# Attention and two FFN layers on one core: float64 words to float32 in two VectorE operations, with a leaky relu for the rescaling

## The chip, the cores and the metric

The kernel runs on one core of a Trainium2 chip. The metric is the device time of one execution in microseconds (us), as the median of several runs. The engines are named as in the profile: PE is TensorE's matmul and PEld its weight load, DVE is VectorE, ACT is ScalarE, POOL is GpSimd, SP is SyncE, which here only issues transfers.

## The reference, cut to what matters

Three layers follow each other. The attention pools keys and values over eight positions, and its result, 4608 tokens of 512 features, goes through two feed-forward layers:

```python
x = attention(q, pooled(k), pooled(v))        # 4608 x 512
h = np.maximum(x @ w_in, 0.0)                 # 512 x 2048
x = (s * (h * h) + b) @ w_out                 # 2048 x 512
gate = 1.0 / (1.0 + np.exp(-(x @ w_gate)))    # 512 x 1536
out = (gate * (x @ w_val) @ w_out2).astype(np.float32)
```

The five weight matrices arrive as float64, the rest as float32.

## The kernel before, in words

The tokens are nine blocks of 512. For the first layer, five blocks (0, 1, 2, 4, 6) go through `emit_h` and `emit_x`, one group of 128 hidden columns at a time (16 groups a block, so 80 steps), and the other four go in pairs through `first_half`, `second_half` and `emit_o`, where seven half-sized products take the place of eight; all of the second layer goes that way too. Each matmul is made of three: the operands are split by `split` (L55, L56) into a rounded high part, which ACT writes, and a remainder, which DVE (for activations) or POOL (for weights) subtracts.

No operation of the kernel works on float64. A weight arrives as 64-bit words in a `raw` tile (128 x 512 of them, 512 KB, loaded by SP at L73), and `convert` makes float32 of it. It sees the tile as two strided views, `low` and `high`, of 32-bit words. ACT reads `high` as a float32 and multiplies it by 2^-112 into `w` (L86), which sets the exponent to the float32 bias and leaves room for a shift. DVE shifts `low` right by 29 in place (L87), then shifts `w` left by 3 and joins the three bits of `low` (L88), which pushes out the sign, and at last takes the sign bit of `high` and joins it (L89). The converted weight then goes to `split`.

There are 68 conversions. Of these, 32 are the 16 groups of `w_in` and of `w_out`, which `split_wi` and `split_wo` convert during block 0, when each step of PE needs a new group of both; the other 36 are weights of the second layer, converted ahead of use by `prep_gate`, `prep_val` and `prep_out`: 12 of them between other work of the first layer's later blocks, 24 in the first layer's paired blocks.

The order of instructions on an engine: the opening (attention of the first two units and the first conversions) stands in the order of the code. From there a planner at build time orders the engines by its own estimates of cost, and from step 16 on PE, and to the end of the steps SP, keep the order of the code, while DVE, ACT and POOL stay with the planner. `raw` has three buffers, so a load waits until a conversion three earlier is done with its tile.

Of the kernel before, what the change touches and what calls it, by code (L numbers as in the profile page):

```python
# [8 lines left out]
F32 = mybir.dt.float32  # L9
F32R = mybir.dt.float32r  # L10
I32 = mybir.dt.int32
ACTF = mybir.ActivationFunctionType
ALU = mybir.AluOpType
# [6 lines left out]
def pooled_attention_two_ffn(ctx, tc, q, k, v, v_left, w_in, w_out, s_in, b_in, w_gate, w_val, w_out2, out):  # L20
# [8 lines left out]
    nc = tc.nc  # L29
# [49 lines left out]
    def convert(raw, w):  # L79

        words = raw.rearrange("p (f two) -> p f two", two=2)
        low, high = words[:, :, 0], words[:, :, 1]
        nc.scalar.activation(out=w.bitcast(F32), in_=high.bitcast(F32), func=ACTF.Copy, scale=2.0**-112)  # L86
        nc.vector.tensor_scalar(out=low, in0=low, scalar1=29, scalar2=None, op0=ALU.logical_shift_right)  # L87
        nc.vector.scalar_tensor_tensor(out=w, in0=w, scalar=3, in1=low, op0=ALU.logical_shift_left, op1=ALU.bitwise_or)  # L88
        nc.vector.scalar_tensor_tensor(out=w, in0=high, scalar=-(2**31), in1=w, op0=ALU.bitwise_and, op1=ALU.bitwise_or)  # L89
        return w.bitcast(F32)  # L90

    def block_of(t):
# [42 lines left out]
    def split_wi(i):  # L135
        if i >= M1:
            return
        w = convert(wi_raw.pop(i), cv_tile())
        t = wi_tile(i)
        split(t[:, 0], t[:, 1], w, nc.gpsimd)  # L140
        later.append((w1d[i], t))
        later.append((w6d[i // 2][:, 0:512] if i % 2 else w6d[i // 2][:, 512:1024], w))
# [12 lines left out]
    def split_wo(m):  # L155
        if m < M1:
            t = wo_p.tile([128, 2, DM], F32R, name=f"wo{m}")
            split(t[:, 0], t[:, 1], convert(wo_raw.pop(m), cv_tile()), nc.gpsimd)
            wo[m] = t
# [11 lines left out]
    def prep_gate(m):  # L171
        prep["gt"] = convert(prep["g"], cv_tile())
# [750 lines left out]
```

## Time and profile before

| | us |
|---|---|
| median of 3 runs | 1774.92 |
| lowest and highest run | 1774.47 and 1777.0 |
| the profiled execution | 1777.24 |
| its span, first to last instruction | 1775.4 |
| PE busy | 1718.1 |
| PEld busy | 1435.0 |
| DVE busy | 996.1 |
| ACT busy | 873.2 |
| POOL busy | 702.8 |

The span is what the trace shows, and 1.84 us lie around it. Busy times of different engines overlap. The mean granted clock of PE over the span is 0.988 of full speed.

### The profile page before, as it was taken

How to read it: one execution, taken by the hardware profiler on the slowest of the kernel's cores; microseconds unless marked ns; L12 is line 12 of the kernel's file. 1: busy time of each engine (PE TensorE's matmuls, PEld its weight loads, DVE VectorE, ACT ScalarE, POOL GpSimd, SP SyncE). 2: the span in 40 equal slices, each digit the busy share in tenths (PEclk: the TensorE clock that was granted, in tenths of full speed). 3: DMA queues.
4: the chain of work that ended last, by engine and by line, in shares of the span. 5: the costliest groups of instructions: out<-in, count | busy, mean ns of one | idle time of the engine just before them, and what ended most of it. 6: DMA issues, size and time to landing. Idle time of an engine off the chain costs nothing.

```text
span 1775.4 us, 22857 instructions
## 1 busy us (share of the span) xinstructions
PE 1718.1 (97%) x8184; PEld 1435.0 (81%) x8184; DVE 996.1 (56%) x1621; ACT 873.2 (49%) x1628; POOL 702.8 (40%) x788
## 2 busy tenths in 40 slices
PE   5889999999999999999999999999999999999998
PEld 4777888788888878877888888888888888888898
DVE  7997555646642597469554454554455444545354
ACT  3666565556555666436653443344434343444244
POOL 4764335455310266336431434133413431443264
PEclk7999999999999999999999999999999999999999
DMA  6876558887444567687475334633463347233753
GB/s 240 298 239 217 180 209 314 276 289 247 175 160 129 197 247 257 228 288 248 173 242 170 117 127 158 222 119 123 152 235 119 110 148 251 102 118 138 250 183 122
DMA packets 98433, 347.01 MB, mean 195 GB/s; under 512 B 11408, under 2 KB 16528, under 8 KB 98320
## 3 DMA queue, kind: packets, MB, share of 16 engines
q1 hardware_dynamic: 90512, 319.33, 52.4%
q0 software_dynamic: 7808, 26.22, 4.2%
q8 instruction: 65, 1.06, 0.2%
q14 instruction: 48, 0.39, 0.1%
HBM read 278.40 MB, written 67.11 MB: 195 GB/s over the span
## 4 chain that ended last, share of the span: by engine, by line
PE 53%; DMA 4%; DVE 2%; issue 2%; POOL 2%; ACT 0%; DVEq 0%; POOLq 0%; SPq 0%; ACTq 0%
PE acc L819 20%; PE pc L723 6%; PE pc L724 6%; PE pc L725 6%; PE pb L725 5%; PE pb L724 5%; PE pb L723 5%; DMA wo<-wo2d 1%; DMA raw<-in 1%; POOL w L56 1%; DMA cv<-x1d 1%; POOL raw L180 1%; DVE raw L87 0%; DMA wo2d<-raw 0%; DVE cv L88 0%
## 5 line engine op out<-in xcount | busy, mean ns | idle before, releaser
L56 POOL TENSOR_TENSOR w<-w 128x256 fp32r<-128x256 f32 (+1 forms) x380 | 369.7, 1006 | 607.6 <-ACT w L55 579.3
L729 DVE TENSOR_TENSOR wk<-pc,wk 128x512 f32<-128x512 f32 (+1 forms) x304 | 196.2, 645 | 319.5 <-PE pc L725 318.9
L723 PE MATMUL pc<-xo,w 128*128 128x512 f32 (+1 forms) x608 | 228.4, 376 | 9.1 <-DVE wk L729 8.9
L724 PE MATMUL pc<-xo,w 128*128 128x512 f32 (+1 forms) x608 | 227.0, 373 | 0.0
L725 PE MATMUL pc<-xo,w 128*128 128x512 f32 (+1 forms) x608 | 226.9, 373 | 0.0
L55 ACT ACTIVATE w<-w 128x256 fp32r<-128x256 f32 (+1 forms) x380 | 157.5, 490 | 100.0 <-DMA w<-w7d 90.9
L56 DVE TENSOR_TENSOR gl<-g,gh 128x512 fp32r<-128x512 f32 (+1 forms) x172 | 133.1, 774 | 96.6 <-ACT gh L55 91.0
L723 PE MATMUL pb<-xo,w 128*128 128x512 f32 (+1 forms) x456 | 169.9, 373 | 1.4 <-ACT g L752 1.1
L725 PE MATMUL pb<-xo,w 128*128 128x512 f32 (+1 forms) x456 | 170.0, 373 | 1.1 <-POOL w L56 1.1
L724 PE MATMUL pb<-xo,w 128*128 128x512 f32 (+1 forms) x456 | 169.8, 372 | 0.0
L55 ACT ACTIVATE gh<-g 128x512 fp32r<-128x512 f32 (+1 forms) x172 | 105.7, 615 | 124.4 <-DVE g L744 122.0
L819 PE MATMUL acc<-wo,s 128*128 128x512 f32 x648 | 150.7, 390 | 0.9 <-DMA wo<-wo2d 0.6
L819 PEld LDWEIGHTS acc<-wo,s 128*128 128x128 f32 x648 | 121.3, 188 | 27.7 <-DMA wo<-wo2d 2.5
L723 PEld LDWEIGHTS pc<-xo,w 128*128 128x128 f32 x608 | 114.9, 189 | 33.4 <-DVE wk L729 13.6
L223 PE MATMUL hps<-xl,wi 128*128 128x512 f32 (+1 forms) x328 | 132.8, 405 | 3.1 <-ACT wi L55 2.5
L819 PE MATMUL acc<-wo,gh 128*128 128x512 f32 x432 | 133.1, 389 | 0.0
L725 PEld LDWEIGHTS pc<-xo,w 128*128 128x128 f32 x608 | 114.9, 189 | 20.3
L724 PEld LDWEIGHTS pc<-xo,w 128*128 128x128 f32 x608 | 115.0, 189 | 19.6
L251 PE MATMUL acc<-gl,wo 128*128 128x512 f32 x320 | 128.4, 401 | 2.4 <-DVE gl L56 2.4
L225 PE MATMUL hps<-xh,wi 128*128 128x512 f32 (+1 forms) x328 | 129.3, 394 | 0.0
L224 PE MATMUL hps<-xh,wi 128*128 128x512 f32 (+1 forms) x328 | 128.8, 393 | 0.0
L253 PE MATMUL acc<-gh,wo 128*128 128x512 f32 x320 | 125.3, 392 | 0.0
(126 smaller groups left out, 3415.4 us busy)
## 6 DMA issues: line engine op xcount, KB each, us to landing
wo<-wo2d SPq DMA_DIRECT2D x108, 512.0 KB, 4.0
w<-w7d SPq DMA_DIRECT2D x60, 896.0 KB, 4.4
raw<-in SPq DMA_DIRECT2D x68, 512.0 KB, 4.8
wi<-w1d SPq DMA_DIRECT2D x64, 512.0 KB, 4.0
wo<-wo1d SPq DMA_DIRECT2D x64, 512.0 KB, 4.6
w<-w6d SPq DMA_DIRECT2D x16, 896.0 KB, 5.9
kv<-in SPq DMA_DIRECT2D x24, 512.0 KB, 6.3
kv<-in SPq DMA_DIRECT2D x16, 576.0 KB, 6.0
```

The source lines that it names most:

```text
L55: nc.scalar.activation(out=hi, in_=src, func=ACTF.Copy)
L56: eng.tensor_tensor(out=lo, in0=src, in1=hi.bitcast(F32), op=ALU.subtract)
L223: nc.tensor.matmul(out=ps[:, f], lhsT=hi[:, kk], rhs=c[:, kk, f], start=kk == 0, stop=False)
L224: nc.tensor.matmul(out=ps[:, f], lhsT=hi[:, kk], rhs=a[:, kk, f], start=False, stop=False)
L225: nc.tensor.matmul(out=ps[:, f], lhsT=lo[:, kk], rhs=a[:, kk, f], start=False, stop=kk == KD - 1)
L251: nc.tensor.matmul(out=acc[j][d], lhsT=hi[:, f], rhs=gl, start=m == 0, stop=False)
L253: nc.tensor.matmul(out=acc[j][d], lhsT=lo[:, f], rhs=gh, start=False, stop=m == M1 - 1)
L723: nc.tensor.matmul(out=ps, lhsT=w[:, 0, x, kk], rhs=r[:, 1, kk, :n], start=first and kk == 0, stop=False, skip_group_check=True)
L724: nc.tensor.matmul(out=ps, lhsT=w[:, 0, x, kk], rhs=r[:, 0, kk, :n], start=False, stop=False, skip_group_check=True)
L725: nc.tensor.matmul(out=ps, lhsT=w[:, 1, x, kk], rhs=r[:, 0, kk, :n], start=False, stop=kk == 1, skip_group_check=True)
L729: nc.vector.tensor_tensor(out=o, in0=ps, in1=b_, op=ALU.add)
L819: nc.tensor.matmul(out=a, lhsT=l, rhs=r, start=m == 0 and first == 0, stop=m == M - 1 and first == 2)
```

## The change

In `convert` the rescaling on ACT becomes a leaky relu with slope 2^32 for negative inputs: a negative word comes out 2^32 times larger than a positive one of the same size, which sets one more bit of its exponent. The shift left by 3 moves that bit into the sign's place. So the DVE operation that fetched the sign from `high` (L89) falls away. Nothing else is edited; `high` is read by ACT alone now.

```diff
         words = raw.rearrange("p (f two) -> p f two", two=2)
         low, high = words[:, :, 0], words[:, :, 1]
-        nc.scalar.activation(out=w.bitcast(F32), in_=high.bitcast(F32), func=ACTF.Copy, scale=2.0**-112)
+        nc.scalar.activation(out=w.bitcast(F32), in_=high.bitcast(F32), func=ACTF.Prelu, scale=2.0**-112, alpha=2.0**32)
         nc.vector.tensor_scalar(out=low, in0=low, scalar1=29, scalar2=None, op0=ALU.logical_shift_right)
         nc.vector.scalar_tensor_tensor(out=w, in0=w, scalar=3, in1=low, op0=ALU.logical_shift_left, op1=ALU.bitwise_or)
-        nc.vector.scalar_tensor_tensor(out=w, in0=high, scalar=-(2**31), in1=w, op0=ALU.bitwise_and, op1=ALU.bitwise_or)
         return w.bitcast(F32)
```

## Rows read from the trace of the kernel before

**Rows 1.** Page, part 1: busy time, share of the span, instructions.

```profile
PE 1718.1 (97%) x8184; PEld 1435.0 (81%) x8184; DVE 996.1 (56%) x1621; ACT 873.2 (49%) x1628; POOL 702.8 (40%) x788
```

**Rows 2.** Windows: stretch, its length, busy time by engine, granted clock, transfers.

```profile
50.00:96.00 46.00, 36.40 (x191) 29.18 (x192) 44.53 (x60) 28.57 (x53) 36.98 (x30) 0.97 0.88 311
96.00:150.00 54.00, 50.21 (x229) 41.19 (x228) 50.25 (x76) 38.20 (x68) 29.14 (x26) 0.90 0.71 237
150.00:600.00 450.00, 444.70 (x2309) 375.95 (x2308) 238.29 (x446) 263.29 (x467) 160.96 (x200) 1.00 0.63 214
600.00:850.00 250.00, 239.84 (x1038) 194.62 (x1037) 177.92 (x242) 145.86 (x255) 135.09 (x145) 0.99 0.73 252
850.00:1776.00 926.00, 918.65 (x4281) 768.77 (x4279) 450.83 (x724) 381.46 (x756) 320.87 (x355) 1.00 0.47 160
```

**Rows 3.** Timeline of TensorE, 74 to 135 us: start, duration, idle before, releaser.

```profile
74.06 0.50 PE L251 MATMUL acc<-gl,wo 128*128 128x512 f32 x1 [2.41 <-DVE gl L56]
...
95.02 0.66 PE L445 MATMUL tl<-ident,lt 128*128 128x128 f32 x2 [3.57 <-DVE lt L423]
...
134.46 1.09 PE L439 MATMUL tm<-ident,pm 128*128 128x128 f32 x4 [2.64 <-DVE e L395]
```

**Rows 4.** Timeline of VectorE, 89 to 95 us.

```profile
89.63 1.42 DVE L89 SCALAR_TENSOR_TENSOR cv<-raw,cv 128x512 int32<-128x512 int32 x1
90.97 1.49 DVE L87 TENSOR_SCALAR raw<-raw 128x512 int32<-128x512 int32 x1
92.39 1.76 DVE L56 TENSOR_TENSOR gl<-g,gh 128x512 fp32r<-128x512 f32 x1
94.07 0.81 DVE L423 TENSOR_TENSOR lt<-pl,lt 128x128 fp32r<-128x128 f32 x1
```

**Rows 5.** Groups by line and shape, VectorE, whole span: count, busy, mean ns.

```profile
L89 DVE SCALAR_TENSOR_TENSOR cv<-raw,cv 128x512 int32<-128x512 int32 x68 | 59.5, 881 | 0.8
```

**Rows 6.** Windows of L89 alone: VectorE's time in it, clock, transfers.

```profile
50.00:96.00 46.00, 8.94 (x9) 0.97 0.88 311
96.00:150.00 54.00, 10.82 (x14) 0.90 0.71 237
600.00:850.00 250.00, 22.05 (x24) 0.99 0.73 252
```

**Rows 7.** Timeline of all engines around the first conversion's end.

```profile
32.09 1.42 DVE L89 SCALAR_TENSOR_TENSOR cv<-raw,cv 128x512 int32<-128x512 int32 x1
...
33.54 0.63 ACT L55 ACTIVATE wi<-cv 128x512 fp32r<-128x512 f32 x1 [5.78 <-DVE cv L89]
...
36.27 0.56 PE L223 MATMUL hps<-xl,wi 128*128 128x256 f32 x1
```

**Rows 8.** Timelines of VectorE and TensorE, two stretches after 650 us.

```profile
656.21 2.01 DVE L89 SCALAR_TENSOR_TENSOR cv<-raw,cv 128x512 int32<-128x512 int32 x1
...
659.48 0.50 PE L723 MATMUL pc<-xo,w 128*128 128x512 f32 x1 [1.48 <-DVE wk L729]
...
791.72 0.69 DVE L88 SCALAR_TENSOR_TENSOR cv<-cv,raw 128x512 int32<-128x512 int32 x1 [1.83 <-ACT cv L86]
...
793.07 0.79 PE L723 MATMUL pc<-xo,w 128*128 128x512 f32 x1 [2.99 <-DVE wk L729]
...
806.86 3.83 DVE L87 TENSOR_SCALAR raw<-raw 128x512 int32<-128x512 int32 x1 [0.90 <-DMA raw<-in]
...
811.34 0.50 PE L723 MATMUL pc<-xo,w 128*128 128x512 f32 x1 [2.83 <-DVE wk L729]
```

**Rows 9.** Groups by line and shape, ScalarE, whole span.

```profile
L229 ACT ACTIVATE g<-g,b_sb,s_sb 128x512 f32<-128x512 f32 x80 | 65.1, 814 | 1.5
L228 ACT ACTIVATE g<-g 128x512 f32<-128x512 f32 x80 | 50.4, 630 | 1.7
L86 ACT ACTIVATE cv<-raw 128x512 f32<-128x512 f32 x68 | 45.0, 669 | 37.9 <-DMA raw<-in 27.4 <-DMA x2d<-eo 5.8 <-POOL raw L56 1.6
L398 ACT ACT_TABLE_LOAD x1 | 1.3, 1283 | 0.7 <-PEq L914 0.7
```

**Rows 10.** The attention's exponential (L398) alone, 0 to 175 us: count, starts.

```profile
L398 ACT ACTIVATE e<-e x9: 682/684/686, 11.0 to 170.7; 128x576 f32<-128x576 f32 x9
```

## The prediction

> **What bounds the kernel now.** I read the page's busy times first: PE is busy for 1718.1 us, 97% of the span [rows 1]. PE's work is the same after the change, so the time can only come out of PE's idle moments and of matmuls that run at a low granted clock. The next view is therefore the windows by stretch, to see where the idle moments lie. From 850 us on PE is busy for 918.65 of 926 us and no conversion runs there any more; from 150 to 600 us it is busy for 444.70 of 450 [rows 2]. What is left lies in two places. From 50 to 150 us, where block 0 needs two new weight groups for each step, PE is idle for 9.60 us (46 less 36.40) and 3.79 us (54 less 50.21), and from 600 to 850 us, the paired blocks with the last 24 conversions, for 10.16 us (250 less 239.84) [rows 2].
>
> In the first of these places the engine that is full is DVE: 44.53 of 46 us and 50.25 of 54 [rows 2]. The timeline of PE says the same: it has ten idle moments between 50 and 138 us, the largest 2.41, 3.57 and 2.64 us long, nine of them ended by a result of DVE [rows 3]. The reader should follow the one of 3.57 us. PE waits for the small `lt` of L423, which takes 0.81 us but starts only at 94.07; ahead of it in DVE's queue stand an L89 of 1.42 us, an L87 of 1.49 and a remainder of L56 of 1.76 [rows 4]. PE pays for the length of the queue and not for the one operation it waits for.
>
> **The change part by part.** *Removed: L89.* It runs 68 times, 59.5 us of DVE in all, 881 ns each [rows 5]. By place: 8.94 us from 50 to 96, 10.82 from 96 to 150, and 22.05 from 600 to 850 [rows 6]; the rest, 17.7 us, lies in the opening and between 150 and 600, where I take it as covered by PE, which is busy for 98.8% of that stretch [rows 2].
>
> *The opening.* The first conversion stands on the path itself: L89 starts at 32.09 and takes 1.42 us, ACT's split follows at 33.54, and the first matmul on that weight starts at 36.27 [rows 7]. Without L89 all of that can start 1.42 us sooner. I take 1.4; the end below is 0, if another of its operands, which come from the attention, is late next.
>
> *50 to 96 us.* PE waits for a full queue, so a stall can shrink by as much as has been taken out of the queue ahead of it: at most 8.94 us of 9.60. At least nothing, because the transfers are busy for 88% of the stretch and POOL for 36.98 of 46 us [rows 2], and either can be what is late next. I take half, 4.5. The stretch right behind it shows that PE can do better when transfers are at 71% [rows 2].
>
> *96 to 150 us.* Here 10.82 us are taken out against 3.79 of idle PE [rows 2, 6], so all of it can go; I take 3.8, with 0 as the other end.
>
> *The clock.* After the long waits PE runs slow: the mean granted clock is 0.97 and 0.90 in the two stretches [rows 2]. Between the levels 2.4 and 1.2 GHz these means are 2.8 us (46 x 0.03 x 2) and 10.8 us (54 x 0.10 x 2) at the lower one, 13.6 in all. If all of that was matmul time, half of it, 6.8 us, is lost; if the two long waits of 3.57 and 2.64 us [rows 3] lie inside it, (13.6 - 6.2) / 2 = 3.7 is lost. A wait that shrinks without vanishing may bring the clock down all the same, so the bounds are 0 and 6.8; I take 2.
>
> *600 to 850 us.* L89 has 22.05 us there [rows 6]. Some waits of PE stand right behind one, as the 1.48 us after an L89 that took 2.01 [rows 8]. But the two largest do not: the 2.99 us follow an L88 that waited 1.83 us for ACT's rescaling, and the 2.83 us follow an L87 that took 3.83 us [rows 8], and these operations stay. That leaves 10.16 - 2.99 - 2.83 = 4.3 us that can go at most; I take 3, with 0 below.
>
> *Changed: the rescaling on ACT.* No row shows a leaky relu. From below it costs nothing more: L86 takes 669 ns, and an operation of the same size without tensor operands for scale and bias 630. From above it costs what two such operands add, 814 - 630 = 184 ns [rows 9]. I take nothing more, as scale and slope are constants in the code. Even 184 ns on the 23 conversions from 50 to 150 us are 4.2 us of ACT, which is busy for 66.8 of these 100 us [rows 2, 6]; and each conversion's chain still gets shorter, by 881 - 184 ns. Without that cover they would cost the 4.2 us.
>
> *Moved by it.* `raw` is free once L88 is done, some 0.9 us sooner, so SP's next load starts sooner; in the stretch at 88% transfers that is no more bytes, only the same ones pressed together. L88 now is the last step of a conversion and may wait for ACT with DVE's whole queue behind it: on DVE stand the remainders `gl` and the attention's reductions, for which PE waits.
>
> *The sum.* 1.4 + 4.5 + 3.8 + 2 + 3 = 14.7 us. The profiled execution took 1777.24 us, which gives 1762.5. The median before is 2.3 us lower, 1774.92, which gives 1760.2. I say 1761. The least of all terms together is nothing, the most 1.4 + 8.9 + 3.8 + 6.8 + 4.3 = 25.2.
>
> **The rivals.** *Transfers and POOL take DVE's place.* For it speaks the 88%, with 311 GB/s, against 237 GB/s behind it [rows 2]; against it, that DVE is at 97% there and that the waits of PE name it. Then 50 to 96 us give 1 or so and the clock nothing. With 1.4 for the opening and some 2 from the other two places that is 4.4, within 2 to 7 us: 1768 to 1773.
>
> *DVE's new order makes it wait (slower).* The planner orders DVE, ACT and POOL anew from its estimates. With a shorter queue it may put an L88 or L87 ahead of an addition of L729 before its input has come, as at 791.72, where 1.83 us of waiting cost PE 2.99 [rows 8]. The trace has two such places. The 24 late conversions have a chance each; five more at 2.9 us eat up the 14.7, and from six on the change loses: with seven, 20.3 - 14.7 = 5.6 us, 1780.
>
> *The leaky relu needs another table.* ACT loads a table in 1283 ns [rows 9], and the exponential, which runs 9 times by 175 us [rows 10], might not share one with it. Then each can cost two loads between the rescalings, at most 18 loads or 23.1 us, and with them ACT would come from 66.8 to some 90 of 100 us: ACT then is late next and eats up the gain, 1775 to 1785. Against it: the kernel's copies, squares and relus run between the exponentials without a load of their own [rows 9].
>
> The Trainium skill bears on this rival: "ScalarE: Activation LUTs", section "Table sets: the hidden batching unit", says that functions are loaded in named sets, that cheap ones such as relu and copy are in every set, and does not list the leaky relu among them. It puts a switch at about 2.7 us with its drain; by that the 18 loads would be an estimated 49 us, more than ACT's 33 idle ones, and the time near 1790, while the trace shows 1283 ns for the load itself.
>
> *The change does not do what it says*, if the freed DVE time goes only where PE was busy anyway. Then the time stays within 2 us of 1774.92.
>
> **How the numbers follow.** Within 0.2%, 3.55 us, a change of this kernel can't be told from none. Chances: the forecast, 7 to 25 us gained, 0.66; transfers and POOL 0.17, of which a bit over half gains more than 3.55 us; no effect 0.05; DVE's new order 0.08, of which 0.05 is slower by more than 3.55 us; the table 0.04, all counted as slower. So faster 0.66 + 0.09 = 0.75, same 0.08 + 0.05 + 0.03 = 0.16, slower 0.09. The likeliest case has 1750 to 1768 for itself; the range reaches down to 1752 and up over the first rival to 1773.5, which leaves out the last cases and the extreme of the first.
>
> **What would show it.** DVE must have 1553 instructions, 68 fewer, with no third conversion step, and some 936 us busy. From 50 to 150 us PE's idle time falls from 13.4 to about 5 us and its granted clock rises over 0.95; the wait for `lt` is gone or below 1 us. The first matmul of L223 starts near 34.9 us. The table loads stay two, and the rescaling stays near 669 ns. What makes the prediction wrong: waits of PE in the same stretch that now name a transfer or POOL, more waits of L88 for ACT after 600 us, or PE's idle time coming back between 150 and 600 us, where the order of the engines may change without any need.

## The result, and the profile after

| | before | after |
|---|---|---|
| median, four runs of each on one chip, us | 1775.58 | 1753.99 |
| lowest and highest, us | 1774.47 and 1777.0 | 1749.55 and 1755.71 |
| the profiled execution, us | 1777.24 | 1752.58 |
| its span, us | 1775.4 | 1750.5 |

The ratio of the two on record, worked out from all runs, is 0.9869, with a 95% interval from 0.9846 to 0.9891: faster by 1.3%. By the medians (ratio 0.988) it is 21.6 us, where 14 were forecast. The time lies inside the range, near its lower end. The experiments below ran on other chips, where the kernel before took 1779.2 to 1781.0 us, so they are compared by their ratios.

The page's busy times of the changed kernel answer to [rows 1]; its lines from L89 on have numbers one lower than before, so L729 is now L728.

```profile
PE 1710.3 (98%) x8184; PEld 1434.1 (82%) x8184; DVE 949.3 (54%) x1553; ACT 872.0 (50%) x1628; POOL 689.5 (39%) x788
```

DVE has the forecast 1553 instructions. It is busy for 46.8 us less, not 59.5. Two things make up the difference. By the groups the other operations got dearer, together by 6.4 us, above all the remainders `lt` of L422 (653 ns in the mean where they took 518, 4.9 us in all) and L87 (717 ns where it took 672, 3.2 us). And the 59.5 us are a sum of durations that overlap a little with their neighbours (the L89 of [rows 4] ends at 91.05, the L87 behind it starts at 90.97), which busy time does not count twice. The groups by shape show the three operations of a conversion that are left (count, busy, mean ns of one, idle before and its releasers), and ACT's two table loads [rows 5, 9]:

```profile
L88 DVE SCALAR_TENSOR_TENSOR cv<-cv,raw 128x512 int32<-128x512 int32 x68 | 55.7, 823 | 15.2 <-ACT cv L86 13.2 <-DMA raw<-in 0.3
L87 DVE TENSOR_SCALAR raw<-raw 128x512 int32<-128x512 int32 x68 | 48.8, 717 | 41.1 <-DMA raw<-in 41.0
...
L86 ACT ACTIVATE cv<-raw 128x512 f32<-128x512 f32 x68 | 44.9, 667 | 24.7 <-DMA raw<-in 19.4 <-issue 4.5 <-DMA x2d<-eo 0.4
...
L397 ACT ACT_TABLE_LOAD x1 | 1.3, 1283 | 0.7 <-PEq L913 0.7
L742 ACT ACT_TABLE_LOAD x1 | 1.3, 1283 | 0.0
```

The rescaling takes 667 ns as a leaky relu against 669 as a copy, and the tables are still loaded twice in all. The windows of [rows 2], for the changed kernel:

```profile
50.00:96.00 46.00, 44.25 (x243) 36.74 (x243) 38.27 (x53) 31.33 (x59) 36.82 (x34) 1.00 0.92 327
96.00:150.00 54.00, 50.24 (x230) 41.46 (x230) 43.06 (x68) 40.87 (x75) 28.87 (x24) 0.94 0.82 274
150.00:600.00 450.00, 447.99 (x2318) 378.79 (x2317) 224.98 (x425) 266.69 (x475) 160.90 (x204) 1.00 0.63 214
600.00:850.00 250.00, 243.44 (x1071) 200.56 (x1070) 172.25 (x232) 150.12 (x259) 131.03 (x148) 1.00 0.74 254
```

From 50 to 96 us PE's idle time fell from 9.60 to 1.75 us, although the transfers are busier (0.92) and POOL is as busy as before. From 96 to 150 it did not fall: 3.76 us against 3.79. The timeline of PE [rows 3] says why. Of the waits behind DVE's queue that were over 1 us, one is left up to 110 us, of 1.62 at 76.44 for `e`, and a single new one stands in the second window:

```profile
106.28 1.09 PE L386 MATMUL sps<-kbd,qT 128*128 128x144 f32 x3 [3.62 <-DVE xl L56]
```

DVE did that `xl` of L56 at 105.54. Ahead of it, at 102.82, stand two remainders `v1l` that had waited 1.41 us for ACT, and behind them an L87. Read so, this wait starts from a handover between ACT and DVE, and not from a full queue; no run takes the handover away.

Windows by the clock of the run compare different work once one kernel is ahead. The table therefore cuts each kernel at the same events, in us: the first matmul on a hidden layer (L223 before, L222 after), the end of block 0 (the first output copy on ACT, L260 and L259), the first product into `pc` of the paired blocks (L723, L722), and the first sigmoid (L743, L742).

| kernel | opening | block 0 | other steps | paired blocks | second layer |
|---|---|---|---|---|---|
| before | 36.3 | 141.8 | 438.1 | 345.9 | 813.3 |
| after | 36.6 | 128.6 | 434.4 | 338.2 | 812.7 |
| e8, four operations | 37.9 | 157.9 | 440.0 | 356.1 | 812.2 |
| e1, three, leaky relu | 37.1 | 143.0 | 437.1 | 347.8 | 812.4 |
| e7, three, other order | 37.0 | 142.2 | 435.6 | 346.7 | 815.2 |
| e2, two in the first layer only | 36.6 | 127.9 | 435.6 | 345.1 | 813.7 |
| e3, two in the second layer only | 36.8 | 143.2 | 435.9 | 341.9 | 815.1 |
| e4, two, other order | 36.2 | 128.1 | 435.9 | 341.6 | 812.5 |
| e5, one | 32.5 | 118.4 | 434.5 | 339.7 | 812.5 |
| e11, two, dearer rescaling | 35.6 | 130.4 | 434.8 | 341.0 | 813.1 |
| e13, two, first load early | 36.2 | 126.5 | 435.3 | 343.9 | 811.8 |
| e14, two, first conversions late | 34.0 | 133.4 | 435.2 | 343.3 | 812.5 |
| e10, as e11 with a tile more | 35.7 | 127.5 | 435.5 | 345.5 | 825.5 |
| e12, two, with a tile more | 34.7 | 130.7 | 435.0 | 343.7 | 826.5 |

Each row is one profiled execution. Block 0 gives 13.2 of the 24.9 us of span, the paired blocks 7.7, the other steps 3.7. These are the windows of block 0 (length, busy time and count of PE, PEld, DVE, ACT and POOL, granted clock, transfers' share, GB/s), first of the kernel before,

```profile
36.30:178.10 141.80, 124.59 (x602) 102.92 (x601) 120.04 (x179) 92.33 (x166) 81.16 (x70) 0.92 0.71 244
```

then of the changed one, with its paired blocks:

```profile
36.60:165.20 128.60, 119.90 (x603) 100.26 (x602) 97.12 (x150) 90.15 (x167) 76.33 (x70) 0.96 0.78 269
599.60:937.80 338.20, 331.64 (x1461) 273.59 (x1460) 212.46 (x293) 188.65 (x325) 150.57 (x172) 1.00 0.71 245
```

In block 0 PE's idle time fell from 17.2 to 8.7 us, and its busy time by 4.7 us for the same matmuls, with the granted clock up from 0.92 to 0.96, closer to the upper level of 2.4 GHz. DVE's busy time fell by 22.9 us with 29 instructions fewer. DVE went from 85% to 76% of the stretch.

### The profile page after: what moved, and what is told of

The parts are those of the page before. It is cut to its first block, busy times and chain, and to the rows that moved or that the text cites. A ratio compares the mean times of both kernels' runs of the same rounds, so it can differ in the third digit from the quotient of the medians.

```text
span 1750.5 us, 22761 instructions
## 1 busy us (share of the span) xinstructions
PE 1710.3 (98%) x8184; PEld 1434.1 (82%) x8184; DVE 949.3 (54%) x1553; ACT 872.0 (50%) x1628; POOL 689.5 (39%) x788
## 4 chain that ended last, share of the span: by engine, by line
PE 75%; DMA 3%; DVE 3%; POOL 1%; issue 1%; ACT 1%; SPq 0%; DVEq 0%; POOLq 0%; ACTq 0%
PE acc L818 24%; PE pc L722 7%; PE pc L724 7%; PE pc L723 7%; PE pb L724 5%; PE pb L723 5%; PE pb L722 5%; PE acc L250 2%; PE acc L252 2%; PE acc L251 2%; PE hps L222 2%; PE hps L224 2%; PE hps L223 2%; DMA raw<-in 1%; PE sps L386 1%
## 5 line engine op out<-in xcount | busy, mean ns | idle before, releaser
L56 POOL TENSOR_TENSOR w<-w 128x256 fp32r<-128x256 f32 (+1 forms) x380 | 367.8, 1001 | 609.0 <-ACT w L55 608.9
L728 DVE TENSOR_TENSOR wk<-pc,wk 128x512 f32<-128x512 f32 (+1 forms) x304 | 196.1, 645 | 328.1 <-PE pc L724 327.6
L722 PE MATMUL pc<-xo,w 128*128 128x512 f32 (+1 forms) x608 | 227.0, 373 | 4.3 <-DVE wk L728 4.3
L723 PE MATMUL pc<-xo,w 128*128 128x512 f32 (+1 forms) x608 | 226.7, 373 | 0.0
L56 DVE TENSOR_TENSOR gl<-g,gh 128x512 fp32r<-128x512 f32 (+1 forms) x172 | 129.9, 756 | 95.4 <-ACT gh L55 89.7
L722 PE MATMUL pb<-xo,w 128*128 128x512 f32 (+1 forms) x456 | 170.2, 373 | 0.7 <-ACT w L55 0.7
L723 PE MATMUL pb<-xo,w 128*128 128x512 f32 (+1 forms) x456 | 170.2, 373 | 0.0
L722 PEld LDWEIGHTS pc<-xo,w 128*128 128x128 f32 x608 | 115.0, 189 | 25.0 <-DVE wk L728 5.1
L222 PE MATMUL hps<-xl,wi 128*128 128x512 f32 (+1 forms) x328 | 130.7, 399 | 1.2 <-ACT wi L55 1.1
L723 PEld LDWEIGHTS pc<-xo,w 128*128 128x128 f32 x608 | 114.9, 189 | 19.9
L224 PE MATMUL hps<-xh,wi 128*128 128x512 f32 (+1 forms) x328 | 126.8, 387 | 0.0
L223 PE MATMUL hps<-xh,wi 128*128 128x512 f32 (+1 forms) x328 | 126.5, 386 | 0.0
```

What stands on the lines that cost most here:

```text
L56: eng.tensor_tensor(out=lo, in0=src, in1=hi.bitcast(F32), op=ALU.subtract)
L222: nc.tensor.matmul(out=ps[:, f], lhsT=hi[:, kk], rhs=c[:, kk, f], start=kk == 0, stop=False)
L223: nc.tensor.matmul(out=ps[:, f], lhsT=hi[:, kk], rhs=a[:, kk, f], start=False, stop=False)
L224: nc.tensor.matmul(out=ps[:, f], lhsT=lo[:, kk], rhs=a[:, kk, f], start=False, stop=kk == KD - 1)
L722: nc.tensor.matmul(out=ps, lhsT=w[:, 0, x, kk], rhs=r[:, 1, kk, :n], start=first and kk == 0, stop=False, skip_group_check=True)
L723: nc.tensor.matmul(out=ps, lhsT=w[:, 0, x, kk], rhs=r[:, 0, kk, :n], start=False, stop=False, skip_group_check=True)
```

## The experiments

### Is it the operation or the function? e1

The leaky relu stands in L86, and L89 stays.

```diff
-        nc.scalar.activation(out=w.bitcast(F32), in_=high.bitcast(F32), func=ACTF.Copy, scale=2.0**-112)
+        nc.scalar.activation(out=w.bitcast(F32), in_=high.bitcast(F32), func=ACTF.Prelu, scale=2.0**-112, alpha=2.0**32)
```

> The leaky relu, and L89 kept behind it (it sets the same sign bit once more), so that the result is the same and only the function on ACT differs from the kernel before; all engines' instructions stand in the same order as before. Theory (the gain is DVE time and what the planner does with it, the rescaling's function costs nothing): 1775, within 2 us of before, and a rescaling of about 669 ns. Rival (the other function changes something on ACT, by a table load or a dearer operation): a rescaling over 700 ns or more than two table loads, and a time 3 us or more away from before.

Measured: 1779.59 us against 1779.98 of before; the ratio over all runs is 1.0006 (0.9993 to 1.0019). The order of instructions on every engine is that of before. The rescaling's group:

```profile
L86 ACT ACTIVATE cv<-raw 128x512 f32<-128x512 f32 x68 | 45.0, 669 | 38.0 <-DMA raw<-in 30.0 <-DMA x2d<-eo 2.7 <-issue 2.1
```

The function costs and gives nothing that can be told; the change's effect comes with the removal of L89.

### Where does it lie? e2 and e3

`convert` gets an argument `short`; where it is false, the three operations of before stand. In e2 it is true for `w_in` and `w_out` (32 conversions), in e3 for the second layer's weights (36).

```diff
-    def convert(raw, w):
+    def convert(raw, w, short):
...
+        if not short:
+            nc.vector.scalar_tensor_tensor(out=w, in0=high, scalar=-(2**31), in1=w, op0=ALU.bitwise_and, op1=ALU.bitwise_or)
```

> The change made only in the 32 conversions of the first layer's weights; the 36 of the second layer keep three operations. Theory (each place gives its own gain: 13 us in block 0, 3 to 4 in the later steps, 8 in the paired blocks): 1758 to 1763. Rival (the planner's new order of the whole program gave the part above the forecast, so that the places don't add up): a time outside 1756 to 1765, or the gain of this one and of the change in the other 36 alone adding up to less than 16 or more than 28 us.

> The change made only in the 36 conversions of the second layer's weights; the 32 of the first layer keep three operations. Theory: block 0 as before, the paired blocks 8 us shorter and the steps up to 4, 1763 to 1770. Rival (order): paired blocks no shorter than 343 us between the first matmul of their products and the first sigmoid, or a block 0 that differs by over 3 us from before.

Measured: e2 1766.7 us, ratio 0.9927 (0.9906 to 0.9949), some 13 us; e3 1771.84 us, ratio 0.9952 (0.9935 to 0.997), some 8 us. As they stand both times miss what was expected, and e2's lies in its rival's bounds; but those were written for the chip of the result above. By the ratios e2 is at 1762.6 us there and e3 at 1767.1, inside both expectations. In the table e2 has the short block 0 and the long paired blocks, e3 the reverse. Together they are 21.4 us, the effect of the whole change (21.6), so the two places add up, as closely as intervals of 3 to 4 us to either side let one see, and there is no sign that what is won in block 0 is given back later. The paired blocks of e3 are 4.0 us shorter than before, half of the 8 expected:

```profile
615.90:957.80 341.90, 334.22 (x1461) 274.31 (x1460) 212.73 (x293) 188.68 (x325) 151.37 (x172) 1.00 0.71 242
```

### Or is it the order that the planner chose? e4 and e7

The line of L87 is written ahead of L86, in the changed kernel (e4) and in the one before (e7), which makes the planner order DVE and ACT otherwise.

```diff
-        nc.scalar.activation(out=w.bitcast(F32), in_=high.bitcast(F32), func=ACTF.Prelu, scale=2.0**-112, alpha=2.0**32)
         nc.vector.tensor_scalar(out=low, in0=low, scalar1=29, scalar2=None, op0=ALU.logical_shift_right)
+        nc.scalar.activation(out=w.bitcast(F32), in_=high.bitcast(F32), func=ACTF.Prelu, scale=2.0**-112, alpha=2.0**32)
```

> The changed kernel with the shift of the low words written ahead of the rescaling, the same work in another order of the code; TensorE, POOL and SP keep the changed kernel's order, DVE and ACT get another one from the planner. Theory (the time follows from the work taken off DVE, and the order matters little): within 3 us of the changed kernel's 1754. Rival (the order decides the part above the forecast): 1758 or more, or 1750 or less.

> The kernel before with the shift of the low words written ahead of the rescaling, the same work with three operations in another order of the code. Theory (order matters little): within 3 us of the kernel before, ratio 0.998 to 1.002. Rival (an order alone can give or take the part of the gain above the forecast): 5 us or more to either side.

Measured: e4 1755.1 us, ratio 0.9869 (0.9854 to 0.9884), the ratio of the change itself; e7 1779.02 us, ratio 0.999 (0.9976 to 1.0003). The order moves the places a little: e4's paired blocks take 341.6 us where those of the change take 338.2. It does not make the gain.

### How much does each operation cost? e8 and e5

In e8 the kernel before takes the sign bit twice (L89 stands two times). In e5 the changed kernel has no L87, and L88 is a shift alone, so that three low bits of the mantissa are left out and DVE does one operation for each conversion.

```diff
-        nc.vector.tensor_scalar(out=low, in0=low, scalar1=29, scalar2=None, op0=ALU.logical_shift_right)
-        nc.vector.scalar_tensor_tensor(out=w, in0=w, scalar=3, in1=low, op0=ALU.logical_shift_left, op1=ALU.bitwise_or)
+        nc.vector.tensor_scalar(out=w, in0=w, scalar1=3, scalar2=None, op0=ALU.logical_shift_left)
```

> The kernel before with L89 issued twice (the same sign bit set once more), 60 us more DVE work and nothing else. Theory (block 0 is full of DVE work, so there each added microsecond counts: 20 to 28 us; in the paired blocks 5 to 10): 25 to 40 us over the kernel before, ratio 1.014 to 1.022. Rival (transfers or POOL pace block 0 and DVE only fills the time): under 12 us over, ratio under 1.007.

> The changed kernel without the shift of the low words: the converted weight gets its sign, exponent and upper 20 bits, and the low word's three bits are left out; the last step is a shift alone. So a further DVE operation (49 us in all) and part of another are taken away. Theory (with two operations left DVE is busy for only 97 of block 0's 129 us and is hardly the bound there any more, so the next one is worth far less than L89 was): 2 to 8 us below the changed kernel, ratio to the kernel before 0.982 to 0.986. Rival (DVE is still what PE waits for, one operation more gives the same again): 12 us or more below the changed kernel, ratio under 0.980.

Measured: e8 1806.74 us, ratio 1.0149 (1.0134 to 1.0164), 26.5 us slower, of which block 0 has 16.1, less than the 20 to 28 expected, and the paired blocks 10.2. The window of its block 0:

```profile
37.90:195.80 157.90, 129.81 (x602) 104.44 (x601) 143.61 (x210) 91.91 (x166) 85.89 (x70) 0.92 0.66 219
```

e5 takes 1738.81 us, ratio 0.9764 (0.975 to 0.9779), some 41 us faster. From four operations to one, block 0 takes 157.9, 141.8, 128.6 and 118.4 us, while DVE's busy time in it falls by 23.6, 22.9 and 23.9 us: 68, 58 and 43% of what is taken off DVE comes back. The theory that DVE no longer sets block 0 once it has two operations fell: the third step still gives 10.2 us there, where DVE was at 76%. Its windows:

```profile
32.50:150.90 118.40, 115.75 (x603) 98.28 (x602) 73.18 (x120) 90.39 (x168) 73.31 (x71) 0.99 0.80 294
```

PE's idle time is down to 2.7 us and the clock up to 0.99. The paired blocks did not get shorter again (339.7 against 338.2 to 343.9), so there L89 was the last operation that counted, as far as that spread lets one see. The 4.1 us of the opening are taken up in the last experiments. POOL gets faster along with it: for its 70 or 71 instructions in block 0 it is busy for 85.9, 81.2, 76.3 and 73.3 us. So part of the gain may come through POOL; no run parts the two, and the longest waits of PE in block 0 name DVE [rows 3].

### Does ACT have cover? e10, e11 and e12

The scale of the rescaling comes from memory. In e10 it has a tile of its own; in e11 it stands in a fourth column of `mask`, which moves no other tile; e12 is the changed kernel with an unused tile of one column.

```diff
+    sc_sb = const.tile([128, 1], F32, name="sc_sb")
...
-        nc.scalar.activation(out=w.bitcast(F32), in_=high.bitcast(F32), func=ACTF.Prelu, scale=2.0**-112, alpha=2.0**32)
+        nc.scalar.activation(out=w.bitcast(F32), in_=high.bitcast(F32), func=ACTF.Prelu, scale=sc_sb, alpha=2.0**32)
```

> The changed kernel with the rescaling's constant read from a one-column tile, so that each of the 68 rescalings on ACT takes about 92 ns more (half of what the two tile operands of the scaling by s and b add); a constant is written once at the start. Theory (ACT has cover, and a chain 92 ns longer is hidden): within 3 us of the changed kernel, ratio 0.985 to 0.989. Rival (with DVE relieved it is ACT that is late next, so that each addition counts): 4 us or more over the changed kernel, ratio 0.990 or more.

> As the kernel with the rescaling's constant in a tile, but the constant stands in a spare column of the mask tile, so that no other tile moves in SBUF (a tile of its own had moved the weight tiles by 32 bytes). Each rescaling on ACT still takes some 92 ns more than in the changed kernel. Theory (ACT has cover, and the 13 us came from where the tiles lie): within 4 us of the changed kernel, ratio to the kernel before 0.985 to 0.9895, and 811 to 815 us from the first sigmoid to the end. Rival (the dearer rescaling cost the 13 us): ratio 0.992 or more.

> The changed kernel with one more tile of one column, written once at the start and never read; the rescaling is the changed kernel's. All that differs is that the tiles behind it, the seven-part weights among them, lie 32 bytes further while the seven activation tiles stay. Theory (where the tiles lie sets the pace of matmul): 820 to 828 us from the first sigmoid to the end, ratio to the kernel before 0.991 to 0.996. Rival (the tile's place is of no account): the changed kernel's time, ratio 0.985 to 0.989, and 811 to 815 us at the end.

Measured: e10 1769.11 us, ratio 0.994 (0.9925 to 0.9955), which looks as if half of the gain had been eaten up. But in the table its block 0 is as short as ever, and 12.8 us of the loss lie in the second layer, where no conversion runs (some more lies in the paired blocks, where PE is busy for 338.3 us in e10 and 338.1 in e12, against 331.6 in the changed kernel and 332.5 to 336.1 in the other kernels with two operations there and the tiles in place). e11, with the same dearer rescaling and the tiles in their places, takes 1756.89 us, ratio 0.9862 (0.9841 to 0.9882), and e12, with the cheap rescaling and the tiles moved, 1771.98 us, ratio 0.9945 (0.9928 to 0.9962). So the dearer rescaling, in e11

```profile
L86 ACT ACTIVATE cv<-raw,mask 128x512 f32<-128x512 f32 x68 | 51.1, 760 | 27.9 <-DMA raw<-in 17.1 <-DMA w7d<-cv 5.3 <-issue 4.2
```

adds 93 ns and costs nothing that can be told, and the place of the tiles costs 12 to 14 us in the second layer (below, with the hardware). The Trainium skill, "ScalarE: Activation LUTs", section "What ACT_TABLE_LOAD costs", puts a scale taken from a tile at about 93 ns; the trace agrees (760 - 667).

### Why did the opening give nothing? e13 and e14

In the changed kernel's opening a first L87 waits for its load, with the attention's reductions behind it on DVE; it stands there in the kernel before too, at 18.26 with a wait of 2.19 us. All engines, changed kernel:

```profile
19.39 0.43 DVE L87 TENSOR_SCALAR raw<-raw 128x512 int32<-128x512 int32 x1 [2.42 <-DMA raw<-in]
...
31.81 0.55 PE L456 MATMUL pv<-t,v1h 128*128 128x256 f32 x1 [5.84 <-DVE t L56]
...
32.68 0.38 DVE L87 TENSOR_SCALAR raw<-raw 128x512 int32<-128x512 int32 x1
...
33.17 0.69 DVE L88 SCALAR_TENSOR_TENSOR cv<-cv,raw 128x512 int32<-128x512 int32 x1
...
33.89 0.63 ACT L55 ACTIVATE wi<-cv 128x512 fp32r<-128x512 f32 x1 [4.35 <-DVE cv L88]
...
36.62 0.53 PE L222 MATMUL hps<-xl,wi 128*128 128x256 f32 x1
```

In e13 the first weight's load is issued ahead of the values' loads, 3.08 us after the start instead of 6.95:

```diff
+        load_wi(0)
         load_kv(0, "v")
...
-        load_wi(0)
```

> The changed kernel with the load of the first weight group issued ahead of the first values' load, so that it lands sooner. In the opening the first shift of low words waits on DVE for that load, with the attention's reductions behind it (2.42 us in the changed kernel, 2.19 before). Theory (this wait sets when the opening ends, and its spread from run to run hid the 1.4 us forecast for the first conversion): the wait gone, the first matmul of the hidden layer at 33 to 35 us instead of 36.6, 2 to 4 us below the changed kernel, ratio 0.9845 to 0.986. Rival (the values, now later, are late next): within 1 us of the changed kernel or slower, the first such matmul at 36 us or later.

Measured: 1755.37 us, ratio 0.9854 (0.9833 to 0.9874). The total lies in the expected range, which tells little, as the changed kernel's own ratio is 0.9869, and the expected step did not happen: L87 still waits 1.77 us and starts at 18.95, and the first matmul on the hidden layer starts at 36.2. The raw load that is issued at 10.67 in the changed kernel, with a median of 8.7 us to its landing there, lands at about 19.4, just when L87 starts. By the order of the code that load is the one of the first output weight, `load_wo(0)`, so L87 may belong to that later weight. In e14, for the first two input weights and the first output weight, the same work is done in another form, in which both operations stand behind ACT:

```diff
+        if first:
+            nc.vector.tensor_scalar(out=w, in0=w, scalar1=3, scalar2=None, op0=ALU.logical_shift_left)
+            nc.vector.scalar_tensor_tensor(out=w, in0=low, scalar=29, in1=w, op0=ALU.logical_shift_right, op1=ALU.bitwise_or)
+        else:
...
-        w = convert(wi_raw.pop(i), cv_tile())
+        w = convert(wi_raw.pop(i), cv_tile(), i < 2)
...
-            split(t[:, 0], t[:, 1], convert(wo_raw.pop(m), cv_tile()), nc.gpsimd)
+            split(t[:, 0], t[:, 1], convert(wo_raw.pop(m), cv_tile(), m == 0), nc.gpsimd)
```

> The changed kernel, but for the three conversions whose raw loads belong to the opening (the first two input weights and the first output weight) the same two VectorE operations stand in another form: the rescaled tile is shifted left by 3 in place, and then the low word, shifted right by 29, is or-ed in. Both now stand behind ScalarE's rescaling, so that none of them can be put early into VectorE's queue. Theory: in the opening the operation of L87 that waits for its raw load (2.42 us in the changed kernel, 1.77 with the first load issued ahead) is that of a later weight and not of the first one, and holds the attention behind it. Without it the first matmul on the hidden layer starts near 32.5 to 34 us instead of 36.6, and the total falls by 2 to 4 us: 0.983 to 0.985 of the kernel before. Rival: the opening of the kernel without L87 (32.5 us) was short because VectorE had an operation less for each conversion; then the first matmul stays at 35.5 or later and the total at 0.986 to 0.987.

Measured: 1760.45 us, ratio 0.9888 (0.9869 to 0.9906). The opening does what the theory says, 34.0 us instead of 36.6, with the first `pv` matmul at 28.94 instead of 31.81. The total does not: block 0 takes 4.8 us more. The timeline of e14 shows where (L91 is the L87 of the other conversions):

```profile
34.19 0.74 DVE L408 TENSOR_REDUCE sm<-e 128x8 f32<-128x576 f32 x1
...
38.88 0.43 DVE L91 TENSOR_SCALAR raw<-raw 128x512 int32<-128x512 int32 x1 [3.94 <-DMA raw<-in]
39.22 0.16 DVE L409 TENSOR_SCALAR sm<-sm 128x8 f32<-128x8 f32 x1
39.70 0.30 POOL L417 TENSOR_TENSOR pl<-e,sm 128x64 f32<-128x64 f32 x1 [5.71 <-DVE sm L410]
39.95 1.04 POOL L417 TENSOR_TENSOR pm<-e,sm 128x512 f32<-128x512 f32 x1
...
41.05 1.12 PE L442 MATMUL tm<-ident,pm 128*128 128x128 f32 x4 [5.14 <-POOL pm L417]
```

The same trap again, one weight later. An L87 waits 3.94 us for its load, between the sum L408 and the operation L409 on it. POOL waits for DVE, and PE for POOL, 5.14 us. In e5 no operation of DVE reads a raw load, and there the opening is 32.5 us and this stall is absent.

## Why the prediction came out as it did

**The mechanism was right.** PE paid for the length of DVE's queue, and part of what is taken out of the queue comes back. e1 takes out the function as a cause, e4 and e7 the order, e2 and e3 show the two places, and e8 makes both worse by doing the opposite. The rival of transfers and POOL falls: from 50 to 96 us the transfers went up to 92% and 327 GB/s, and PE's idle time still fell by 7.85 us.

**50 to 96 us, 4.5 forecast.** Mis-sized: 7.85 us of PE's idle time went. Halving it for the transfers' share was the error; the upper bound of 8.94 was nearer.

**96 to 150 us, 3.8 forecast.** Nothing came of it in that window, 3.79 to 3.76, since the wait of 3.62 us at 106.28 took the place of the old ones. The step "all of it can go" failed: it counted DVE's queue, and the attention's handovers from ACT to DVE were late next. The wait for `lt` is gone and PE's idle time from 50 to 150 us is 5.5 us, near the 5 forecast. That is luck: one term was too small by 3.4 us and the other too large by 3.8. Over block 0, cut at the events, 8.3 us were forecast by the two and 8.5 came (17.2 to 8.7).

**The clock, 2 forecast.** PE's busy time in block 0 fell by 4.7 us for the same matmuls, as its granted clock rose from 0.92 to 0.96. Mis-sized: the estimate looked only at 50 to 150 us, and block 0 reaches from 36 to 178; up to 50 us its clock was 0.67 before and is 0.86 now. The sign given for it came: the mean from 50 to 150 us rose from 0.93 to 0.97, though from 96 to 150 us alone it is 0.94.

**600 to 850 us, 3 forecast.** PE's idle time in the whole paired blocks fell from 10.2 to 6.6 us, close to the term. The stretch itself is 7.7 us shorter, because PE's busy time is 4.1 us less too, which no term held. The other kernels with two operations there (e3, e4, e11, e13, e14) take 341.0 to 343.9 us, against 345.1 to 347.8 with three (before, e1, e2, e7), so some 4 to 5 us belong to L89 and the rest to this one order or to chance. Of the waits that "stay", the kind did: an L87 held for 7.36 us now makes the largest (DVE, POOL and PE, 630 to 640 us, with L728 the addition that PE waits for):

```profile
630.53 0.75 POOL L179 TENSOR_TENSOR raw<-raw,cv 128x256 f32<-128x256 f32 x1
630.70 7.36 DVE L87 TENSOR_SCALAR raw<-raw 128x512 int32<-128x512 int32 x1 [1.29 <-DMA raw<-in]
631.24 4.62 POOL L56 TENSOR_TENSOR w<-w 128x512 fp32r<-128x512 f32 x5
635.83 1.26 POOL L56 TENSOR_TENSOR raw<-cv,raw 128x512 fp32r<-128x512 f32 x1
637.06 0.71 POOL L179 TENSOR_TENSOR raw<-cv,raw 128x256 f32<-128x256 f32 x1
638.16 0.69 DVE L88 SCALAR_TENSOR_TENSOR cv<-cv,raw 128x512 int32<-128x512 int32 x1
638.77 0.68 DVE L728 TENSOR_TENSOR wk<-pc,wk 128x512 f32<-128x512 f32 x1
...
639.51 0.50 PE L722 MATMUL pc<-xo,w 128*128 128x512 f32 x1 [3.06 <-DVE wk L728]
```

L87 takes 0.43 us in the median; here it lasts through a row of POOL operations without a gap. The Trainium skill, "SBUF — State Buffer", section "SBUF: two separate sides", says that VectorE and GpSimd share a pair of ports as an exclusive lock: of a GpSimd operation and a VectorE one in a two-port mode or with two SBUF inputs, whichever starts first has the pair for its whole instruction, and the other blocks. The rows fit in that L87 ends only when POOL's row has ended. Whether L87 is such an operation, and why it would not get in between two operations of POOL, no row shows, and no run here takes POOL's work away.

**150 to 600 us, nothing forecast.** The other steps took 3.7 us less in the profile; over the kernels with two operations there (e3, e4, e11, e13, e14, after) it is 434.4 to 435.9 us, against 435.6 to 438.1 with three. Near nothing, as said.

**The opening, 1.4 forecast.** In this pair it measured nothing: 36.3 us before, 36.6 after. From the first `pv` matmul to the first on the hidden layer the path did get shorter, from 6.26 to 4.81 us, by the 1.4 us that were worked out. But the `pv` matmuls start at 31.81 instead of 30.01, so the gain is gone ahead of that; 1.1 of these 1.8 us come from a load that an L87 waits for there (L87 starts at 19.39 instead of 18.26). Over all kernels some of it may show: the openings take 36.3 to 37.1 us with three operations in the first layer (before, e1, e3, e7) and 34.7 to 36.6 with two (after, e2, e4, e10 to e13), in the mean 36.8 and 35.9. The text ahead of the prediction has the opening in the order of the code, but on DVE an L87 of the work behind the opening stands among its operations: that of the first output weight, whose L88 is one of the two that run from 40.52, some 21 us later. What the term had wrong is the path: it took the first conversion's end as what counts, and left out a load that the attention's operations stand behind. e14 gives 2.6 us against the changed kernel without that wait, and shows how much the later order depends on such waits.

**The other rivals.** The table rival falls: two loads. "DVE's new order" did bring new waits, of 3.62 and 3.06 us, but no more than the old order had, and the other orders of e4 and e7 moved the total by 0.1% or less, which is within their intervals. L88's waits for ACT grew from 8.5 to 13.2 us over the span, but not after 600 us (2.1 to 1.8), where they were named as a sign of being wrong; the large waits of PE name other operations.

What stays open: why block 0 gives another 10.2 us in e5. The missing L87 and the simpler L88 take away 24 us of DVE's work and 6.3 us of its waits for raw loads at once, and no run parts the two. Open too is what share of the gain in block 0 goes by way of POOL.

## What to carry to other kernels

Where an in-order engine's queue feeds the matmuls, look at what is queued ahead of the operation that is waited for. Taking an operation out of that queue paid here by about two thirds to two fifths of its busy time in block 0, the less the less full the engine was; and at 76% busy the engine still counted, so its share alone did not tell when it stopped to matter. Cut the spans of two kernels at the same events before comparing stages, since windows of the same times hold different work. An operation that waits for a load holds up everything behind it on its engine, as in the opening and in e14, so what a planner puts early is to be read from the trace and not from the code.

## What the runs showed of the hardware that was not expected

An unused tile of one column (e12) moves the tiles allocated behind it, the product's weights among them, by 32 bytes, while the moving operands `xo` keep their place. The second layer then takes 826.5 us instead of 812.7. Its windows, first of the changed kernel,

```profile
937.80:1750.50 812.70, 807.04 (x3786) 677.39 (x3784) 396.82 (x643) 327.33 (x663) 291.38 (x322) 1.00 0.45 154
```

then of e12:

```profile
944.10:1770.60 826.50, 820.75 (x3786) 677.19 (x3784) 398.19 (x643) 329.79 (x663) 290.75 (x322) 1.00 0.45 151
```

PE's idle time is the same (5.66 and 5.75 us), the granted clock is the same, and the matmuls themselves take 13.7 us more. By shape (second layer, first two groups of the changed kernel, then the same of e12):

```profile
L818 PE MATMUL acc<-wo,s 128*128 128x512 f32 x648 | 149.9, 390 | 0.0
...
L722 PE MATMUL pc<-xo,w 128*128 128x512 f32 x380 | 147.9, 389 | 0.0
...
L724 PE MATMUL pc<-xo,w 128*128 128x512 f32 x380 | 150.3, 396 | 0.0
...
L820 PE MATMUL acc<-wo,s 128*128 128x512 f32 x648 | 149.9, 389 | 0.0
```

The products, whose weights moved while `xo` stayed, take 396 ns instead of 389; the output's matmuls, whose two operands moved together, take the same time. There are 1986 products of this shape in the second layer, and 7 ns each are 13.9 us. e10 and e11, which differ in the place of the tiles too, give 825.5 and 813.1 us. Which distance between the operands is a good one, and by what mechanism, was not tried; that a change of one column in a tile's list can be worth more than half of this case's gain is reason enough to keep the tiles in place when operations are compared.
